# q and k loaded three tokens to a partition, and all loads in one order, in an attention and feed-forward kernel

## The chip, the cores and the metric

The kernel runs on one core of one Trainium2 chip. The time is that of the device, in microseconds (us), for one execution of the whole program: from inputs in HBM to the output in HBM. Besides plain timed runs there is one execution recorded by the hardware profiler, which gives the views quoted here. Engines are named as in the profile: PE does matmuls (and transposes), PEld is its loading of weights, DVE, ACT and POOL work on tensors, SP here only issues transfers (DMAs). ACT and POOL can issue DMAs too.

## The reference

Attention with a window of 128 tokens and four sink tokens, for 4 batches, 8 heads, 768 tokens and 64 dimensions a head, then a feed-forward layer over the 3,072 tokens. Cut to what matters:

```python
def _attn_ref(q, k, v, n_sink, window):      # n_sink 4, window 128
    scores = scale * np.matmul(q, k.transpose(0, 1, 3, 2))
    keep = is_sink | in_window               # rel >= 0 and rel < window
    scores = np.where(keep, scores, -1000000000.0)
    a = np.exp(scores - np.max(scores, axis=-1, keepdims=True))
    a = a / (np.sum(a, axis=-1, keepdims=True) + 1e-09)
    return np.matmul(a, v)

def _moe_ref(x, w_in, w_out, beta):          # x: 3072 x 512
    h = x @ w_in                             # 512 x 2048
    g = h * (1.0 / (1.0 + np.exp(-beta * h)))
    return g @ w_out                         # 2048 x 512
```

All inputs and the output are float32. The kernel works in bfloat16 between them.

## The kernel before

**Blocks and units.** The 3,072 tokens are cut into eight blocks of 384 (`HALF`; half a sequence). The attention of a block has four units, one for each pair of heads, so there are 32 units `u`; block `hb` is `u // 4`. The feed-forward layer works on whole blocks `T_`.

**Stages.** `load` brings q, k and v of a block into staging tiles (`stg`, two sets) in float32. `cast` makes bfloat16 of them: `x16` for q and k, `vaug` for v, which has a column of ones for the sum of the softmax. Stage T transposes q and k of a unit on PE (six 128 x 128 transposes, L417) and copies the result out of PSUM into `qkT` (L423, the copies appear at L306 for DVE and L308 for ACT); for the first block of a sequence it also copies the four sink columns of k into `kS` (L429). SC makes the scores of five or six 128 x 128 blocks (L468), ACT their exponentials (L478), POOL sets what lies outside the window to zero (L484), and DVE handles the sink blocks (L492). SS makes the scores against the sink tokens for the others (L502, L505). AV multiplies with `vaug` and `vS` (L530, L540) and divides (L544, L546). OT transposes back into `xT` (L558). H multiplies `xT` with `w_in` (L578), ACT takes the tanh (L582), DVE forms `g` (L584). O multiplies `g` with `w_out` over 16 steps (L596), the sum is copied to `osb` and stored by SP (L607).

**Who decides the order.** Each engine executes its instructions in the order in which the program adds them, and waits on semaphores. That order is worked out when the kernel is built: `Graph` keeps a modelled time for each engine and for the DMA engines (`free`, `dma_free`, `HOP` for a semaphore), each `add` has a modelled duration, and the loop at the end always adds the stage that can start earliest on PE, attention stages before feed-forward ones. `background` adds the next load when the modelled DMA backlog is under 3,000 ns, and the next cast when its data are due. `quickest` picks the engine for copies and for some casts, by the modelled times.

**Loads before.** In block 0, one DMA per head for q, k and v, q and v on SP and k on ACT, in the order q, k, v for each pair of heads. In the other blocks, one DMA of 256 KB for each 128 tokens of q, k or v, all heads, on SP. In both, token `c * 128 + p` lies in partition `p`, so each run in HBM is one token of one head, 64 float32 or 256 B. The weights come in eight chunks of 1 MB each (read as float32, written as bfloat16, 512 KB), issued by POOL: `w_in` after block 0, `w_out` after block 1. A DMA waits only until the tile that it writes is free.

**Names the prediction uses.** L352 issues loads of q, k and v, L361 those of the weights, L397 are the casts on POOL, L406 the copies of the sink rows of v.

Of the kernel before, what the change touches and what calls it, by code (L numbers as in the profile page):

```python
# [26 lines left out]
class Graph:  # L27
# [5 lines left out]
    HOP = 130  # L33

    def __init__(self):
        self.ops = []
        self.writers = {}
        self.readers = {}
        self.last_x = {}
        self.n_dma = 0  # L40
        self.n_eng = {e: 0 for e in self.ENGINES}
        self.free = {e: 0.0 for e in self.ENGINES}
        self.dma_free = 0.0

    def add(self, eng, fn, ns=0, r=(), w=(), x=(), dma=None):

        o = Op()
        o.eng, o.fn, o.dma = eng, fn, dma
        o.signal, o.count, o.waits, o.vc = False, 0, [], None
        o.seq = self.n_eng[eng]  # L50
        self.n_eng[eng] += 1
        deps = []
        for k in r:
            ws = self.writers.get(k)
            assert ws, k
            deps += [(p, True) for p in ws.values()]
        for k in w:
            deps += [(p, False) for p in self.readers.get(k, {}).values()]
            deps += [(p, False) for p in self.writers.get(k, {}).values()]
        for k in x:  # L60
            deps += [(p, False) for p in self.last_x.get(k, {}).values()]
        o.deps = deps
        who = ("dma", self.n_dma) if dma else eng
        if dma:
            self.n_dma += 1
        for k in r:
            self.readers.setdefault(k, {})[who] = o
        for k in w:
            self.writers[k] = {who: o}
            self.readers[k] = {}  # L70
        for k in x:
            self.last_x.setdefault(k, {})[eng] = o
        at = self.free[eng]
        for p, _ in deps:
            at = max(at, p.end + (0 if p.eng == eng and not p.dma else self.HOP))
        if dma:
            self.free[eng] = at + (1150 if eng == "gp" else 550)
            self.dma_free = max(self.dma_free, at + 900) + ns
            o.end = self.dma_free + 900
        else:  # L80
            o.end = self.free[eng] = at + ns
        self.ops.append(o)
        return o
# [144 lines left out]
def _program(nc, G, sb, ps, q, k, v, w_in, w_out, beta, out):  # L228
# [8 lines left out]
    hbeta = sb("hbeta", (128, NM), F32)  # L237
    xT = sb("xT", (128, 4, NTOK), BF16)
    w_in16 = sb("w_in16", (128, 4, DF), BF16)
    w_out16 = sb("w_out16", (128, NM, NOUT), BF16)  # L240
    stg = {n: sb(n + "_stage", (128, NK, H, D), F32, NSTG) for n in "qkv"}
# [14 lines left out]
    def add(eng, fn, ns, r=(), w=(), x=(), dma=None):  # L256
        return G.add(eng, fn, ns, r, w, x, dma)

# [71 lines left out]

    def beta_in():
        b_ = take(1)
        add("pe", lambda e: nc.tensor.transpose(P[:, b_[0], 0:NM], beta_st[:, :], ident32[:, :]), 30,
            r=["beta_st", "ident32"], x=[("B", b_[0])])
        add("dve", lambda e: e.tensor_scalar(hbeta[:, :], P[:, b_[0], 0:NM], 0.5, None, ALU.mult), 80,
            w=["hbeta"], x=[("B", b_[0])])
        give(b_)


    def load(hb, n, c, hp):  # L340

        b, t0, z = hb // 2, hb % 2 * HALF, hb % NSTG
        t = {"q": q, "k": k, "v": v}[n]
        if hp is None:
            src = t[b, :, t0 + c * 128:t0 + (c + 1) * 128, :].rearrange("h p d -> p h d")
            jobs = [(stg[n][z][:, c, :, :], src, [(n, z, c, i) for i in range(4)], f"d{n}{z}{c}", 262144)]
        else:
            jobs = [(stg[n][z][:, :, h, :], t[b, h, t0:t0 + HALF, :].rearrange("(c p) d -> p c d", p=128),
                     [(n, z, i, hp) for i in range(NK)] if h % 2 else [("first", n, hp)],
                     f"h{n}{h}", 98304) for h in (2 * hp, 2 * hp + 1)]  # L350
        for i, (dst, src, keys, sem, nbytes) in enumerate(jobs):
            add("act" if hp is not None and n == "k" else "sp", lambda e, dst=dst, src=src: e.dma_start(dst, src),  # L352
                nbytes / 265, w=[("stg",) + k_ for k_ in keys], dma=sem)

    def load_w(j):

        if j < 4:
            dst, src = w_in16[:, :, j * 512:(j + 1) * 512], w_in_src[:, :, j * 512:(j + 1) * 512]
        else:
            dst, src = w_out16[:, 4 * (j - 4):4 * (j - 3), :], w_out_src[:, 4 * (j - 4):4 * (j - 3), :]  # L360
        add("gp", lambda e: e.dma_start(dst, src), 1048576 / 380,  # L361
            w=[("w16", j)], dma=f"dw{j}")

    def cast(hb, n, c, hp):
        z = hb % NSTG
        cs = slice(0, NK) if c is None else slice(c, c + 1)
        hs = slice(0, H) if hp is None else slice(2 * hp, 2 * hp + 2)
        keys = [(i, j) for i in (range(NK) if c is None else [c]) for j in (range(4) if hp is None else [hp])]
        src = stg[n][z][:, cs, hs, :]
        r = [("stg", n, z) + k_ for k_ in keys]  # L370
        if hp is not None:
            r.append(("stg", "first", n, hp))
        if n == "v":
            dst = vaug[hb % NV][:, cs, hs, 0:D]
            w = [("v", hb % NV) + k_ for k_ in keys]
            r.append(("vones", hb % NV))
        else:
            dst = x16[n][hb % NX][:, cs, hs, :]
            w = [(n + "16", hb % NX) + k_ for k_ in keys]
        nc_, nh = (NK if c is None else 1), (H if hp is None else 2)  # L380
        opts = {}
        if n != "v" or nc_ == 1:
            opts["gp"] = pool_ns(nc_ * nh * D, nc_ * nh)
        if hb == 0:
            opts["dve"] = dve_ns(nc_ * nh * D)
            opts["act"] = act_ns(nc_ * nh * D) + 90
        eng = quickest(opts)
        if eng == "gp":
            if n == "v":
                dst, src = dst[:, 0, :, :], src[:, 0, :, :]  # L390
                patt = [[0, nh], [0, D]]
            else:
                dst, src = (a.rearrange("p c h d -> p c (h d)") for a in (dst, src))
                patt = [[0, nc_], [0, nh * D]]
                if nc_ == 1:
                    dst, src, patt = dst[:, 0, :], src[:, 0, :], patt[1:]
            fn = lambda e: e.affine_select(dst, src, patt, ALU.is_ge, 0.0, base=0, channel_multiplier=0)  # L397
# [3 lines left out]
        if n == "v" and hb % 2 == 0 and (hp == 3 or c == 0):  # L401
            z = hb // 2 % 2
            v0 = vaug[hb % NV][0:NSINK, 0, :, :].rearrange("p (a two) d -> p a two d", two=2)
            for hh in range(2):
                dst_ = vS[z][32 * hh:32 * hh + NSINK, :, :].rearrange("p (a two) d -> p a two d", two=2)[:, :, hh, :]
                add("dve", lambda e, dst_=dst_, hh=hh: e.tensor_copy(dst_, v0[:, :, hh, :]), 200,  # L406
                    r=[("vS", z)] + [("v", hb % NV, 0, j) for j in range(4)], w=[("vSd", z, hh)])


    def T(u):  # L410
# [4 lines left out]
        for i, n in enumerate("qk"):  # L415
            for c in range(NK):
# [3 lines left out]
                    mm_ns(128), r=[(n + "16", hb % NX, c, hp), "ident"], x=[("B", bs[0])])  # L420
        opts = {"dve": dve_ns(2 * HALF, 1.92), "act": act_ns(2 * HALF)}
        eng = quickest(opts)
        add(eng, copy_fn(eng, qkT[u % NT][:, :, :].rearrange("p a s -> p (a s)"), mp[:, 0:2 * HALF]), opts[eng],  # L423
            w=[("qkT", u % NT)], x=[("B", bs[0])])
        if hb % 2 == 0:
            ks = u % NKS
            for hh in range(2):
                rows = slice(64 * hh, 64 * hh + 64)
                add(eng, copy_fn(eng, kS[ks][rows, 32 * hh:32 * hh + NSINK], mp[rows, HALF:HALF + NSINK]), 70,  # L429
                    r=[("kS", ks)], w=[("kSd", ks, hh)], x=[("B", bs[0])])  # L430
# [85 lines left out]
    def av_keys(u):  # L516
        z = u % NE
        ks = {(p[0], z, p[1]) for ps in parts(where(u)[1]) for p in ps}
        return sorted(ks) + [("v", u // 4 % NV, c, u % 4) for c in range(NK)] + [("ES", z), ("vSd", u // 8 % 2, 1)]

    def AV(u):
# [4 lines left out]
        for m, ps in enumerate(parts(half)):  # L526
# [8 lines left out]
            for hh in range(2):  # L535
                c0 = (2 * m + hh) * (D + 1)
                for n, (kind, j, i, kb) in enumerate(ps):
# [4 lines left out]
                        r=[(kind, z, j), ("v", vz, kb % NK, hp)], x=[("B", bs[0])])  # L542
# [71 lines left out]
    def xl(hb):  # L614
        return [(hb, n, None, hp) for hp in range(4) for n in "qkv"] if hb == 0 else \
            [(hb, n, c, None) for c in range(NK) for n in "qkv"]

    LOADS = xl(0) + [0, 1, 2, 3] + xl(1) + [4, 5, 6, 7] + [x for hb in range(2, NSB) for x in xl(hb)]
    CASTS = [x for hb in range(NSB) for x in xl(hb)]
# [5 lines left out]
    def head(s):  # L625

        i = done[s]
        if s == "T":
            if i >= NU or i - NT + 4 >= min(done["SC"], done["SS"]):
                return None  # L630
            if n_cast[0] < (3 * i + 2 if i < 4 else 11 + 9 * (i // 4)):
                return None
            t = G.at([(n + "16", i // 4 % NX, c, i % 4) for n in "qk" for c in range(NK)])
# [7 lines left out]
        elif s == "AV":  # L641
            if i >= NU or i >= done["OT"] + NON or i >= min(done["SC"], done["SS"]) or n_cast[0] < (3 * i + 3 if i < 4 else 12 + 9 * (i // 4)):
# [33 lines left out]
    def background():  # L676
# [3 lines left out]
        while moved:  # L680
            moved = False
            i = done["load"]
            if i < len(LOADS) and G.dma_free <= now + BACKLOG:
# [6 lines left out]
                elif x[0] - NSTG < at_hb:  # L690
                    load(*x)
                    for c in range(NK) if x[2] is None else [x[2]]:
                        for hp in range(4) if x[3] is None else [x[3]]:
                            mark(("in",) + x, ("stg", x[1], x[0] % NSTG, c, hp))
# [3 lines left out]
            if i < len(CASTS):  # L698
                hb, n, c, hp = CASTS[i]
                t = G.at([("in",) + CASTS[i]])  # L700
                ok = done["T"] >= 4 * (hb - NX + 1) if n != "v" else done["AV"] >= 4 * (hb - NV + 2)
                if t is not None and ok and t <= now + AHEAD:
                    cast(hb, n, c, hp)
# [3 lines left out]
    add("sp", lambda e: e.dma_start(beta_st[:, :], beta.rearrange("(m p) -> m p", p=128)), 100, w=["beta_st"],  # L707
        dma="dbeta")
    consts()
    for x in xl(0):  # L710
        load(*x)
        for c in range(NK):
            mark(("in",) + x, ("stg", x[1], 0, c, x[3]))
    done["load"] = 12
# [66 lines left out]
```

## Time and profile before

| | us |
|---|---|
| median of 3 runs | 254.6 (253.06 to 254.76) |
| the profiled execution | 254.02 |
| its span, first to last instruction | 252.3 |
| PE busy in the span | 229.4 (91%) |
| ACT, DVE, POOL busy | 160.6, 121.8, 100.3 |
| DMA packets under 512 B, of all | 75,648 of 82,856 |
| bytes moved | 29.70 MB |

In the table by slices each digit is the busy share of one fortieth of the span, in tenths. PEclk is the clock that PE was granted, in tenths of full speed. A DMA share above 1 comes from packets that overlap on one DMA engine. In the chain of waits each line is a start, a length (both us) and what the end of the program was waiting for then. In the tables by group, a line names engine, operation, shapes and count, then busy time in us and mean ns of one, then the idle time of the engine ahead of it and what ended it.

### The profile page before, as it was taken

The numbers are of one execution on the slowest core, as the hardware profiler recorded it, in microseconds if no ns is written. First come the engines' busy times: TensorE is split into PE (matmuls) and PEld (weight loads), VectorE is DVE, ScalarE is ACT, GpSimd is POOL, SyncE is SP. The second block draws the span as 40 slices with busy tenths as digits, with TensorE's granted clock in tenths as the row PEclk, the third lists the DMA queues.
The fourth block names the chain that finished last, engine by engine and source line by source line (L and its number), as shares of the span: only waits on it lengthen the run. The fifth ranks groups of instructions, "written<-read, shape, count | busy, mean of one in ns | idle before, by whom it ended". The sixth has DMA issues, their size and how long they took to land.

```text
span 252.3 us, 5040 instructions
## 1 busy us (share of the span) xinstructions
PE 229.4 (91%) x1889; PEld 132.0 (52%) x1889; DVE 121.8 (48%) x274; ACT 160.6 (64%) x298; POOL 100.3 (40%) x204
## 2 busy tenths in 40 slices
PE   1588955899999999999999999999999999999994
PEld 0364632456565675656557565555555555555531
DVE  0484840244577567645657446533633533343320
ACT  1874873525998967899789776655644655554420
POOL 6582439464895989596298360000000000000000
PEclk9997997799999999999999999999999999999999
DMA  7999999969999899985011010111011011111112
GB/s 165 216 215 199 227 191 224 153 164 225 263 208 238 197 249 221 257 182 145 0 45 44 0 42 3 42 44 42 23 59 48 0 42 44 42 42 42 44 42 83
DMA packets 82856, 29.70 MB, mean 118 GB/s; under 512 B 75648, under 2 KB 79760, under 8 KB 82832
## 3 DMA queue, kind: packets, MB, share of 16 engines
q1 hardware_dynamic: 75408, 24.39, 39.5%
q0 software_dynamic: 4224, 4.19, 10.3%
q10 hardware_dynamic: 3200, 0.79, 1.4%
q8 instruction: 15, 0.25, 0.4%
q14 instruction: 9, 0.07, 0.1%
HBM read 27.27 MB, written 6.29 MB: 133 GB/s over the span
## 4 chain that ended last, share of the span: by engine, by line
PE 66%; SPq 11%; ACT 9%; DMA 7%; DVE 4%; issue 1%; POOL 1%; DVEq 0%
PE P L596 29%; PE P L578 26%; SPq L352 11%; ACT E L478 4%; DMA w_out<-in_moe_w_out_dram 4%; DMA v_stage<-in_v_dram 3%; PE P L540 2%; ACT t L582 2%; PE P L417 2%; PE P L558 2%; PE P L468 2%; DVE g L584 2%; DVE onorm L546 1%; ACT osb L308 1%; PE P L530 1%
## 5 line engine op out<-in xcount | busy, mean ns | idle before, releaser
L584 DVE SCALAR_TENSOR_TENSOR g<-t,P 128x384 bf16<-128x384 f32 x128 | 70.3, 554 | 81.9 <-ACT t L582 63.5
L582 ACT ACTIVATE t<-P,hbeta 128x384 f32<-128x384 f32 x128 | 74.2, 588 | 49.3 <-PE P L578 46.1
L596 PE MATMUL P<-w_out,g 128*128 128x512 bf16 x384 | 98.7, 383 | 6.5 <-DMA w_out<-in_moe_w_out_dram 5.6
L578 PE MATMUL P<-xT,w_in 128*128 128x384 bf16 x512 | 98.4, 330 | 0.4 <-ACT osb L308 0.4
L578 PEld LDWEIGHTS P<-xT,w_in 128*128 128x128 bf16 x512 | 49.2, 99 | 39.2 <-issue 1.5
L484 POOL TENSOR_SCALAR_AFFINE_SELECT E<-E 128x256 bf16<-128x256 bf16 (+1 forms) x112 | 52.0, 499 | 24.6 <-ACT E L478 24.4
L596 PEld LDWEIGHTS P<-w_out,g 128*128 128x128 bf16 x384 | 36.4, 98 | 42.5 <-ACT ES L505 3.6
L478 ACT ACTIVATE E<-P 128x768 bf16<-128x768 f32 x64 | 45.2, 765 | 9.9 <-PE P L468 9.4
L308 ACT ACTIVATE osb<-P 128x512 f32<-128x512 f32 x22 | 13.2, 602 | 14.6 <-PE P L596 14.6
L540 PE MATMUL P<-vaug,E 128*128 128x65 bf16 x352 | 19.8, 199 | 0.0
L397 POOL TENSOR_SCALAR_AFFINE_SELECT vaug<-v_stage 128x512 bf16<-128x512 f32 x21 | 14.0, 667 | 12.7 <-DMA v_stage<-in_v_dram 12.7
L540 PEld LDWEIGHTS P<-vaug,E 128*128 128x128 bf16 x352 | 17.7, 102 | 2.4 <-POOL E L484 0.3
L468 PE MATMUL P<-qkT 64*128 64x128 bf16 (+1 forms) x256 | 16.7, 254 | 2.4 <-ACT qkT L308 1.1
L546 DVE TENSOR_TENSOR onorm<-P,rden 128x384 bf16<-128x384 f32 x32 | 17.8, 558 | 1.1
L505 ACT ACTIVATE ES<-P 128x128 bf16<-128x128 f32 (+1 forms) x32 | 12.0, 400 | 3.9 <-PE P L502 3.6
L308 ACT ACTIVATE xT<-P 128x384 bf16<-128x384 bf16 x23 | 11.4, 500 | 4.5 <-PE P L558 4.4
L468 PEld LDWEIGHTS P<-qkT 64*128 64x128 bf16 x256 | 9.2, 99 | 9.6 <-issue 2.7
L558 PE MATMUL P<-ident,onorm 128*128 128x128 bf16 x96 | 10.9, 223 | 3.0 <-DVE onorm L546 2.3
L530 PE MATMUL P<-vS,ES 128*128 128x130 bf16 x64 | 13.3, 227 | 0.0
L544 DVE RECIPROCAL rden<-P 128x6 f32<-128x6 f32 x32 | 6.1, 191 | 14.0 <-PE P L540 13.7
L306 DVE COPY qkT<-P 128x768 bf16<-128x768 bf16 x20 | 10.8, 553 | 1.7 <-PE P L417 1.5
L558 PEld LDWEIGHTS P<-ident,onorm 128*128 128x128 bf16 x96 | 6.3, 98 | 9.8 <-DVE onorm L546 5.9
(46 smaller groups left out, 130.0 us busy)
## 6 DMA issues: line engine op xcount, KB each, us to landing
out_dram<-osb SPq DMA_DIRECT2D x24, 256.0 KB, 2.0
q_stage<-in_q_dram SPq DMA_DIRECT2D x21, 256.0 KB, 4.7
k_stage<-in_k_dram SPq DMA_DIRECT2D x21, 256.0 KB, 4.6
v_stage<-in_v_dram SPq DMA_DIRECT2D x21, 256.0 KB, 4.8
w_in<-in_moe_w_in_dram POOLq DMA_DIRECT2D x4, 512.0 KB, 8.5
w_out<-in_moe_w_out_dram POOLq DMA_DIRECT2D x4, 512.0 KB, 9.1
k_stage<-in_k_dram ACTq DMA_DIRECT2D x8, 96.0 KB, 4.0
q_stage<-in_q_dram SPq DMA_DIRECT2D x8, 96.0 KB, 3.4
```

The source lines that it names most:

```text
L308: return lambda e: e.activation(dst, src, AF.Copy, bias=0.0, scale=scale)
L352: add("act" if hp is not None and n == "k" else "sp", lambda e, dst=dst, src=src: e.dma_start(dst, src), nbytes / 265, w=[("stg",) + k_ fo ...
L468: add("pe", lambda e, dst=dst, kt=kt, kc=kc, rows=rows, q0=q0, nq=nq: e.matmul(dst, kt[rows, 1, kc:kc + 128], qkT[u % NT][rows, 0, q0:q0 + ...
L478: add("act", lambda e, src=src, dst_=dst_: e.activation(dst_, src, AF.Exp, bias=0.0, scale=SCALE), act_ns(256 * n), w=[(k_, z, j) for k_ i ...
L484: add("gp", lambda e, d=d, sg=sg, at_=at_: e.affine_select(d, d, [[0, 2 * len(at_)], [sg, 128]], ALU.is_ge, 0.0, base=min(sg, 0), channel_ ...
L540: e.matmul(A[:, c0:c0 + D + 1], E[z][:, i, hh, :], vaug[vz][:, kb % NK, 2 * hp + hh, :], start=a, stop=o, skip_group_check=True), 39,
L546: add("dve", lambda e: e.tensor_tensor(onorm[on][:, :, :, :].rearrange("p m h d -> p (m h) d"), av[:, :, 0:D], rden[on][:, :].unsqueeze(2) ...
L558: add("pe", lambda e, m=m: nc.tensor.transpose(mp[:, m * 128:(m + 1) * 128], onorm[on][:, m, :, :].rearrange("p h d -> p (h d)"), ident[:, ...
L578: add("pe", lambda e, c=c: e.matmul(hp, w_in16[:, c, m * 128:(m + 1) * 128], xT[:, c, t0:t0 + HALF], start=(c == 0), stop=(c == 3)), mm_ns ...
L582: add("act", lambda e: e.activation(tt[ti][:, :], hp, AF.Tanh, bias=0.0, scale=hbeta[:, m:m + 1]), act_ns(HALF) + 93, r=["hbeta"], w=[("t" ...
L584: add("dve", lambda e: e.scalar_tensor_tensor(gt[T_ % NG][:, m, :], tt[ti][:, :], 1.0, hp, ALU.add, ALU.mult), dve_ns(HALF), r=[("t", ti)] ...
L596: add("pe", lambda e, m=m: e.matmul(P[:, bk, :], gt[T_ % NG][:, m, t * 128:(t + 1) * 128], w_out16[:, m, :], start=(m == 0), stop=(m == NM ...
```

## The change

q and k are loaded with three neighbouring tokens to a partition: token `3 * p + j` lies in partition `p`, so a run in HBM is three tokens of one head, 768 B. Staging for q and k is laid out head by head (`H, NK, D`). The casts pick out the tokens of one `j`, so that each transpose gives every third token, and the copy out of PSUM writes them back in order, with a step of three elements. The sink copy for `kS` reads `qkT` instead of PSUM. v keeps its layout and its 256 B runs.

In block 0, q and k come in one DMA for each pair of heads (192 KB), then v in three DMAs of 256 KB; only the first k is on ACT, all else on SP. In the other blocks q is one DMA, k is one, v is three. AV of block 0 now waits for all eleven casts of the block. The load of beta moves from the first place on SP to behind six of these DMAs.

`ordered` gives all loads one order, weights too: each waits until the load that lies more than 1,600,000 bytes ahead of it has landed, whichever queue issues it. An early activation (`warm`) is added, and the constants of the model are changed. Keys of the planner follow the new layout.

```diff
-    HOP = 130
+    HOP = 180
...
-        self.free = {e: 0.0 for e in self.ENGINES}
+        self.free = {e: 800.0 for e in self.ENGINES}
...
-            self.dma_free = max(self.dma_free, at + 900) + ns
-            o.end = self.dma_free + 900
+            self.dma_free = max(self.dma_free, at + 1100) + ns
+            o.end = self.dma_free + 1000
...
-    stg = {n: sb(n + "_stage", (128, NK, H, D), F32, NSTG) for n in "qkv"}
+    stg = {n: sb(n + "_stage", (128, H, NK, D), F32, NSTG) for n in "qk"}
+    stg["v"] = sb("v_stage", (128, NK, H, D), F32, NSTG)
...
+    AHEAD_BYTES = 1600000
...
+        add("act", lambda e: e.activation(warm[:, :], ones[0:1, 0:1], AF.Exp, bias=0.0, scale=1.0), 1300,
+            r=["ones"], w=["warm"])
...
+    flight = []
+
+    def ordered(nbytes):
+
+        ahead, wait = 0, []
+        for key, b_ in reversed(flight):
+            ahead += b_
+            if ahead > AHEAD_BYTES:
+                wait = [key]
+                break
+        key = ("flight", len(flight))
+        flight.append((key, nbytes))
+        return wait, [key]
+
+    def load(hb, n, i):
 
         b, t0, z = hb // 2, hb % 2 * HALF, hb % NSTG
...
+        if n == "v":
+            src = v[b, :, t0 + i * 128:t0 + (i + 1) * 128, :].rearrange("h p d -> p h d")
+            dst, keys, ns = stg[n][z][:, i, :, :], [i], 262144 / 240
         else:
...
+            hs = slice(0, H) if i is None else slice(2 * i, 2 * i + 2)
+            src = {"q": q, "k": k}[n][b, hs, t0:t0 + HALF, :].rearrange("h (p j) d -> p h (j d)", j=NK)
+            dst = stg[n][z][:, hs, :, :].rearrange("p h j d -> p h (j d)")
+            keys, ns = ([i], 196608 / 350) if i is not None else (range(4), 786432 / 350)
+        wait, mine = ordered(dst.shape[0] * dst.shape[1] * dst.shape[2] * 4)
+        add("act" if hb == 0 and n == "k" and i == 0 else "sp", lambda e: e.dma_start(dst, src), ns, r=wait,
+            w=[("stg", n, z, j) for j in keys] + mine, dma=f"d{n}{z}{'' if i is None else i}")
...
-        add("gp", lambda e: e.dma_start(dst, src), 1048576 / 380,
-            w=[("w16", j)], dma=f"dw{j}")
...
+        wait, mine = ordered(1048576)
+        add("gp", lambda e: e.dma_start(dst, src), 1048576 / 380, r=wait, w=[("w16", j)] + mine, dma=f"dw{j}")
...
+        elif hb == 0:
+            hs = slice(2 * i, 2 * i + 2)
+            src = stg[n][z][:, hs, :, :].rearrange("p h j d -> p j h d")
+            dst = x16[n][hb % NX][:, :, hs, :]
...
+            src, dst = stg[n][z][:, :, i, :], x16[n][hb % NX][:, i, :, :]
...
-        opts = {"dve": dve_ns(2 * HALF, 1.92), "act": act_ns(2 * HALF)}
+        opts = {"dve": dve_ns(2 * HALF), "act": act_ns(2 * HALF)}
         eng = quickest(opts)
-        add(eng, copy_fn(eng, qkT[u % NT][:, :, :].rearrange("p a s -> p (a s)"), mp[:, 0:2 * HALF]), opts[eng],
+        add(eng, copy_fn(eng, qkT[u % NT][:, :, :].rearrange("p a (s j) -> p a j s", j=NK),
+                         mp[:, 0:2 * HALF].rearrange("p (a j s) -> p a j s", a=2, j=NK)), opts[eng],
             w=[("qkT", u % NT)], x=[("B", bs[0])])
...
-                add(eng, copy_fn(eng, kS[ks][rows, 32 * hh:32 * hh + NSINK], mp[rows, HALF:HALF + NSINK]), 70,
-                    r=[("kS", ks)], w=[("kSd", ks, hh)], x=[("B", bs[0])])
+                add(eng, copy_fn(eng, kS[ks][rows, 32 * hh:32 * hh + NSINK], qkT[u % NT][rows, 1, 0:NSINK]), 70,
+                    r=[("kS", ks), ("qkT", u % NT)], w=[("kSd", ks, hh)])
...
+        if hb:
+            return [(hb, "q", None), (hb, "k", None)] + [(hb, "v", c) for c in range(NK)]
+        return [(0, n, i) for i in range(4) for n in "qk"] + [(0, "v", c) for c in range(NK)]
...
-    CASTS = [x for hb in range(NSB) for x in xl(hb)]
+    CASTS = xl(0) + [(hb, n, i) for hb in range(1, NSB) for n in "qkv" for i in range(NK)]
...
-            if n_cast[0] < (3 * i + 2 if i < 4 else 11 + 9 * (i // 4)):
+            if n_cast[0] < (2 * i + 2 if i < 4 else 8 + 9 * (i // 4)):
...
-            if i >= NU or i >= done["OT"] + NON or i >= min(done["SC"], done["SS"]) or n_cast[0] < (3 * i + 3 if i < 4 else 12 + 9 * (i // 4)):
+            if i >= NU or i >= done["OT"] + NON or i >= min(done["SC"], done["SS"]) or n_cast[0] < 11 + 9 * (i // 4):
```

The list `LOADS` is as before: block 0, four chunks of `w_in`, block 1, four chunks of `w_out`, then the other blocks.

## The prediction

> **What bounds the kernel now.** I read the page's table by slices (6.3 us each) first, then the chain of waits, then busy times in stretches cut where the slices change.
>
> ```profile
> PE   1588955899999999999999999999999999999994
> ...
> PEclk9997997799999999999999999999999999999999
> DMA  7999999969999899985011010111011011111112
> ```
>
> PE is full from about slice 8 (50 us) to the end. Before that it has gaps and a lowered clock, and there the DMA engines are full. The stretches say it in us (PE, PEld, DVE, ACT, POOL busy, clock, DMA share, GB/s):
>
> ```profile
> 0.00:50.20 50.20, 33.36 (x286) 20.07 (x286) 21.51 (x52) 30.38 (x55) 27.91 (x64) 0.90 1.08 200
> 33.00:50.20 17.20, 10.68 (x100) 5.72 (x100) 3.73 (x9) 9.29 (x15) 9.26 (x19) 0.80 1.10 187
> 50.20:60.00 9.80, 9.77 (x78) 5.32 (x79) 3.51 (x10) 2.27 (x4) 5.83 (x11) 1.00 0.72 176
> 60.00:155.00 95.00, 92.68 (x1031) 58.18 (x1029) 58.16 (x145) 80.36 (x158) 66.57 (x131) 1.00 0.62 147
> ```
>
> Up to 50.2 us PE stands idle for 16.8 us, 6.5 of them between 33 and 50.2. From 50.2 to 155 us it is idle for 2.4. So what a load is worth is read from the first 50 us alone: later, other matmuls stand ready whenever a load is late. The chain names the loads:
>
> ```profile
> 16.95 5.81 SPq L352
> 22.80 4.35 SPq L352
> ...
> 29.72 7.90 DMA v_stage<-in_v_dram
> 37.68 0.67 POOL vaug L397
> ...
> 40.95 9.21 DMA w_out<-in_moe_w_out_dram
> 50.21 1.04 PE P L596 x4
> ```
>
> SP itself is held in issuing (5.8 and 4.4 us for one DMA), the last v chunk of block 1 lands at 37.6, and the last of w_out at 50.2, though only then the O stage of block 0 can finish. The queue of transfers, not an engine, ends this stage.
>
> **Loads: the runs.** Up to 50.2 us 10.02 MB were written: 4.19 of weights (eight chunks), 4.72 for blocks 0 and 1, and 1.05 for block 2 (four chunks that SP issued at 30.6, 31.7, 33.2 and 38.6, before or among the w_out chunks). Between 52.5 and 65 us, with no weights, q/k/v moved at 233 GB/s at a DMA share of 0.97. At that rate 5.77 MB take 24.8 us; with 2 us before the first bytes, the weights are left 50.2 - 2 - 24.8 = 23.4 us, 2.9 a chunk.
>
> ```profile
> q1 hardware_dynamic: 75408, 24.39, 39.5%
> 160.00:170.00 10.00, 10.00 (x55) 5.19 (x53) 3.92 (x8) 4.71 (x9) 0.00 (x0) 1.00 0.15 54
> ```
>
> A packet of that queue, nearly all 256 B, costs 0.395 x 252.3 x 16 / 75408 = 21.1 ns. No row has 768 B. Lower bound: as much as one of 256 B, 21.1, as it holds more bytes. Upper bound: as much as the three that it replaces, 63.3. The second row above has only output stores, 2 KB packets: 0.15 x 16 x 10 us / 264 packets = 91 ns. On the line between 256 B and 2 KB, 768 B lies at 41 ns, 0.65 of three; I take that, as it uses both neighbours. q and k of a block, 1.57 MB, then need 4.4 instead of 6.75 us; 2.25 and 6.75 are the ends. v keeps 3.4.
>
> **Loads: the order.** Each load now waits until what is more than 1.6 MB ahead has landed, so block 2 no longer mixes with w_out: 1.05 MB / 233 = 4.5 us. The last w_out chunk lands at 2 + 2 x (4.4 + 3.4) + 23.4 = 41 us instead of 50.2 (36.7 to 45.7 at the ends of the run price); w_in is in at 21.5, block 1 at 29.3 instead of 37.6.
>
> Moving seven of ACT's eight k DMAs to SP leaves one hardware queue. Two together moved 254 GB/s between 2 and 10 us, one 233 later: 0.6 us on 1.57 MB, or nothing. The Trainium skill, DMA: Bandwidth & Descriptors, section Rules for kernel authors, says that spreading DMAs over issuing engines adds no bandwidth, as all feed the same 16 engines; by the rule the price is zero, by the two stretches up to 0.6. I take zero here and keep 0.6. SP issues 11 DMAs for block 0 at about 0.53 us each instead of 17, so issuing ends near 6 us and doesn't limit. ACT loses 3.7 us of issuing, and its table load (1.28 us at 5.06) moves to about 1.4 by the new first activation.
>
> **PE in the first 50 us.** In the order in which the time falls:
> - FFN start. Its first matmul is at 20.3. Block 0's last v cast starts at 13.4 now; the loads would be in at about 9.8, and the first pair of q and k, one DMA each, issued at 0.8, about 1 us earlier. What remains is casts, copies and exps on ACT and DVE: eight casts at 0.53, four qkT copies at 0.8 to 0.95, four times 1.6 of exp, some 3 of masks and kS, 17 us on two engines. AV of the first pair now has to wait for all eleven loads, 9.8 us; it starts at 14.4 anyway. Of the 3.6 us by which loads are earlier I count 2.0 (between 0 and 3.6).
> - The gap. Of the 6.5 us idle between 33 and 50.2, what stays is where block 1 is paced by its four units on POOL (4 masks a unit, 1.94 us, 7.8 in all) and ACT (1.5 + 0.43 a unit). Transposes near 29 and w_out chunks at 32, 35, 38 and 41 give PE 7 us of attention and about 3 to 5 of L596 in the 11 us until then. I count 4.5 saved, 2 left (0 to 6.5).
> - The clock, in stretches of 2.5 us:
>
> ```profile
> 37.50:40.00 2.50, 0.59 (x3) 0.32 (x4) 0.00 (x0) 1.08 (x3) 2.31 (x4) 1.00 1.22 201
> 40.00:42.50 2.50, 1.18 (x11) 0.40 (x10) 0.00 (x0) 1.51 (x2) 2.49 (x6) 0.69 1.25 248
> 42.50:45.00 2.50, 2.50 (x20) 1.52 (x18) 0.00 (x0) 0.00 (x0) 1.16 (x3) 0.50 1.24 211
> 45.00:47.50 2.50, 2.22 (x16) 0.92 (x14) 1.11 (x3) 1.95 (x3) 0.77 (x2) 0.50 1.22 198
> ```
>
> Behind a stretch with 0.59 us of work PE runs at 0.69 and 0.50: 1.18 x 0.31 + (2.50 + 2.22) x 0.5 = 2.7 us lost. Half is saved, 1.4.
>
> **What is added on engines.** The qkT copy writes every third element:
>
> ```profile
> L306 DVE COPY qkT<-P 128x768 bf16<-128x768 bf16 x20 | 10.8, 553 | 1.7 <-PE P L417 1.5
> L308 ACT ACTIVATE qkT<-P 128x768 bf16<-128x768 bf16 x12 | 10.0, 829 | 1.5 <-PE P L417 1.5
> L584 DVE SCALAR_TENSOR_TENSOR g<-t,P 128x384 bf16<-128x384 f32 x128 | 70.3, 554 | 81.9 <-ACT t L582 63.5
> ```
>
> DVE packed: 768 elements 553 ns, 384 (the xT copy) 358, so 0.51 ns an element and 162 fixed. At L584's rate, (554 - 162) / 384 = 1.02, it is 945. Bounds 553 and 945; I take 945. The Trainium skill, VectorE: DVE Perf Modes, section What auto-detection actually checks, speaks against the change: two 16-bit results a cycle need step 1. Its table of cycles makes an estimate of 925 ns, and no row here has the strided copy; the sum by it is the same to 0.4 us. On DVE 20 x 0.39 = 7.8 us more, of which 6 fall into 60 to 155, where DVE has 37 idle: hidden. If DVE were full it would cost the 6. ACT keeps 829 or less, as its row shows no faster packed form. POOL's casts of q/k go from 615 to v's 667, 42 x 0.05 = 2.2 us, in 28 us of idle. The kS copies now read qkT and wait for their own engine's copy, 153 ns each; SS and the exps queue behind: at most 32 x 0.1. I take +0.5 for all these.
>
> SP's new waits stand ahead of loads and, after 50 us, of output stores; four osb buffers cover some us. POOL's stand ahead of casts and masks: see the second rival. Planner constants reorder everything else; no row prices that, and I put it in the range as 1 us either way.
>
> **Sum.** -2.0 - 4.5 - 1.4 + 0.5 = -7.4. The profiled execution took 254.0 (span 252.3 and 1.7 around it): 246.6. It lies 0.6 below the median of 254.6: about **247.0** in the median. Changes under 1% (252.1 to 257.1) are what a measurement can't tell from none.
>
> **Rivals.**
> - *Only the order helps.* 768 B cost 63 ns, or the runs are cut into 256 B packets after all: w_out at 45.7, half of the first three terms, 254.6 - 3.9 + 0.5 = 251.2. For it: no row shows such a packet. Against: 2 KB costs 91, not eight times 21.1.
> - *POOL's queue paces the loads: slower.* A weight chunk takes 8.5 to 9.1 us from issue to landing now, and the new wait lets two be in flight. At 8.8, eight chunks need 4 x 8.8 = 35 us instead of 23.4, w_out ends at 52.7, its last issue is at 43.9 instead of 41.0, and the masks of block 1 are behind it on POOL. The 16.9 us from that issue to the first L578 of block 1 (57.8) then end 3 us later: 254.6 + 3 + 0.5 = 258. It decides from about 8 us a chunk. Against: 8.8 includes q/k/v sharing the engines; two chunks alone are 5.9.
> - *ACT takes the copies.* If all go to ACT, 15 x 0.81 = 12 us join its 80.4 of 95: 97%, and masks and tanh wait. With 6 us lost the gain is nearly gone: 253.2. Against: DVE has room.
>
> **How the numbers follow.** Forecast 0.60 (243 to 249.5), order only 0.15, ACT 0.11, POOL 0.14. Faster by over 1%: 0.60 + 0.15 = 0.75 and a little of ACT, 0.76; within: 0.11; slower: 0.13. The range goes from 241.5 (all of 3.6, 6.5 and 2.7) to 254, which leaves out POOL and the ends of the others.
>
> **What would show it.** Packets on q1 near 45,500 instead of 75,408 (24,576 of q and 21,504 of k go, a third of 48,384 comes); last w_out landing at 41; first L578 near 18; idle PE from 33 to 50 us under 3; DVE's qkT copy near 945 ns. I'm wrong if w_out chunks still take over 8 us from issue, or POOL's masks wait behind them, or PE gets new idle after 60 us with ACT ahead of it.

## The result, and the profile after

The changed kernel takes 264.3 us (261.97 to 265.0), the kernel before 253.83 in the same session: a ratio of 1.0395, with an interval of 1.0315 to 1.0475. It is slower by 4%, where 247.0 was forecast. Here and below a time is the median of all executions, while a ratio compares means and leaves out executions more than 1.5% above the fastest of their kernel. The profiled execution has a span of 263.2 us, 10.9 more than before.

The first view is the page's table by slices of the changed kernel (6.6 us each here).

```profile
PE   1688977597899699988999999999999999999995
...
DMA  6799995999999990970010101011111111111112
```

Counted from slice 0, PE has gaps up to slice 18 now (125 us); before, it was full from slice 8 (50 us). The DMA engines have a gap in slice 6 (39 to 46 us), while the weights are still on their way. The stretches say where the time is (columns as before: length, PE, PEld, DVE, ACT, POOL, clock, DMA share, GB/s):

```profile
10.00:15.00 5.00, 3.85 (x32) 1.68 (x31) 4.20 (x8) 4.97 (x12) 3.46 (x8) 1.00 0.45 75
33.00:50.20 17.20, 11.94 (x136) 6.84 (x134) 6.79 (x14) 13.66 (x20) 12.80 (x24) 1.00 0.93 161
60.00:155.00 95.00, 85.47 (x892) 51.16 (x890) 62.14 (x130) 82.53 (x143) 62.25 (x119) 0.98 0.57 144
```

From 60 to 155 us PE is idle for 9.5 us, against 2.3 before. This is the stretch in which the prediction let other matmuls stand ready. Between 33 and 50.2 it is idle for 5.3 instead of 6.5. The idle time after 60 us is not the whole loss: over the whole span PE's idle time rose from 22.9 to 28.4 us, and its busy time from 229.4 to 234.8 for the same 1,889 matmuls; why these got longer isn't shown. The row from 10 to 15 us shows the DMA engines at 0.45 (0.94 before): they run dry in the stage that they were to end. Two groups of the page (engine, operation, shapes, count, then busy us and mean ns) name the engines' new work:

```profile
L313 ACT ACTIVATE qkT<-P 128x768 bf16<-128x768 bf16 x20 | 28.8, 1486 | 1.1 <-PE P L427 1.1
...
L311 DVE COPY qkT<-P 128x768 bf16<-128x768 bf16 x12 | 17.4, 1448 | 0.4 <-PE P L427 0.4
```

The copy that puts q and k back in order takes 1,486 ns on ACT, which had 829, and 1,448 on DVE, which had 553. In all, 46.2 us of copies where there were 20.8. In the page's shares of the chain that ended last, by engine and by line, they are the largest item behind the two feed-forward matmuls, 9% and 2% of the span; before, no such copy was among the fifteen largest, and ACT had 9% in all.

```profile
PE 64%; ACT 21%; DVE 6%; DMA 4%; issue 1%; POOL 1%; SPq 0%; DVEq 0%; ACTq 0%
PE P L589 28%; PE P L607 26%; ACT qkT L313 9%; ACT E L489 6%; PE P L551 3%; DMA w_out<-in_moe_w_out_dram 3%; PE P L569 2%; ACT t L593 2%; PE P L479 2%; DVE g L595 2%; DMA k_stage<-in_k_dram 2%; DVE qkT L311 2%; DVE onorm L557 2%; ACT ES L516 1%; PE P L427 1%
```

The chain of waits of the changed kernel, cut to the stage that the prediction was about (start, length, what the end waited for):

```profile
35.18 3.90 ACT qkT L313 x3
...
42.33 1.89 POOL E L495 x4
44.21 6.62 DMA w_out<-in_moe_w_out_dram
50.89 1.46 PE P L607 x3
```

Three copies in a row lead it, then exps and the masks of a unit, then the last chunk of w_out, which POOL issues only behind these masks. It lands at 50.8 us; before, 50.2. So two things went wrong, and the experiments have to say how far they belong together: the copies became slower than was priced, and the faster loads didn't bring the weights in any earlier.

### The profile page after: what moved, and what is told of

Same layout as the page of the kernel before. It is cut to its first block, busy times and chain, and to the rows that moved or that the text cites. A ratio compares the mean times of both kernels' runs of the same rounds, so it can differ in the third digit from the quotient of the medians.

```text
span 263.2 us, 4995 instructions
## 1 busy us (share of the span) xinstructions
PE 234.8 (89%) x1889; PEld 132.6 (50%) x1889; DVE 132.6 (50%) x267; ACT 179.1 (68%) x307; POOL 100.5 (38%) x202
## 3 DMA queue, kind: packets, MB, share of 16 engines
q1 hardware_dynamic: 44912, 24.98, 35.6%
## 4 chain that ended last, share of the span: by engine, by line
PE 64%; ACT 21%; DVE 6%; DMA 4%; issue 1%; POOL 1%; SPq 0%; DVEq 0%; ACTq 0%
PE P L589 28%; PE P L607 26%; ACT qkT L313 9%; ACT E L489 6%; PE P L551 3%; DMA w_out<-in_moe_w_out_dram 3%; PE P L569 2%; ACT t L593 2%; PE P L479 2%; DVE g L595 2%; DMA k_stage<-in_k_dram 2%; DVE qkT L311 2%; DVE onorm L557 2%; ACT ES L516 1%; PE P L427 1%
## 5 line engine op out<-in xcount | busy, mean ns | idle before, releaser
L589 PE MATMUL P<-xT,w_in 128*128 128x384 bf16 x512 | 100.0, 333 | 0.4 <-DVE rden L555 0.4
L589 PEld LDWEIGHTS P<-xT,w_in 128*128 128x128 bf16 x512 | 50.0, 100 | 39.2 <-issue 3.3
L313 ACT ACTIVATE qkT<-P 128x768 bf16<-128x768 bf16 x20 | 28.8, 1486 | 1.1 <-PE P L427 1.1
L551 PE MATMUL P<-vaug,E 128*128 128x65 bf16 x352 | 20.9, 203 | 0.2 <-ACT vaug L313 0.2
L313 ACT ACTIVATE osb<-P 128x512 f32<-128x512 f32 x20 | 12.1, 604 | 12.3 <-PE P L607 12.3
L479 PE MATMUL P<-qkT 64*128 64x128 bf16 (+1 forms) x256 | 17.8, 251 | 2.2 <-ACT E L489 0.9
L551 PEld LDWEIGHTS P<-vaug,E 128*128 128x128 bf16 x352 | 18.5, 104 | 2.3 <-issue 0.6
L557 DVE TENSOR_TENSOR onorm<-P,rden 128x384 bf16<-128x384 f32 x32 | 17.8, 558 | 1.1
L311 DVE COPY qkT<-P 128x768 bf16<-128x768 bf16 x12 | 17.4, 1448 | 0.4 <-PE P L427 0.4
L516 ACT ACTIVATE ES<-P 128x128 bf16<-128x128 f32 (+1 forms) x32 | 12.9, 409 | 1.0 <-PE P L513 0.8
```

The source lines that it names most:

```text
L311: return lambda e: e.tensor_copy(dst, src)
L313: return lambda e: e.activation(dst, src, AF.Copy, bias=0.0, scale=scale)
L479: add("pe", lambda e, dst=dst, kt=kt, kc=kc, rows=rows, q0=q0, nq=nq: e.matmul(dst, kt[rows, 1, kc:kc + 128], qkT[u % NT][rows, 0, q0:q0 + ...
L551: e.matmul(A[:, c0:c0 + D + 1], E[z][:, i, hh, :], vaug[vz][:, kb % NK, 2 * hp + hh, :], start=a, stop=o, skip_group_check=True), 39,
L557: add("dve", lambda e: e.tensor_tensor(onorm[on][:, :, :, :].rearrange("p m h d -> p (m h) d"), av[:, :, 0:D], rden[on][:, :].unsqueeze(2) ...
L589: add("pe", lambda e, c=c: e.matmul(hp, w_in16[:, c, m * 128:(m + 1) * 128], xT[:, c, t0:t0 + HALF], start=(c == 0), stop=(c == 3)), mm_ns ...
```

## The experiments

The theories: COPY (the step on the writing side makes the copies slow, and that makes the kernel slow), ORDER (the loads' new waits do), PLAN (an order that the planner made with wrong durations does), and, for the missing gain of the loads, POOL, MIX and CHANCE. Each ratio is to the kernel before, run beside it.

**1. The same copy, walked in the other order.**

```diff
-        add(eng, copy_fn(eng, qkT[u % NT][:, :, :].rearrange("p a (s j) -> p a j s", j=NK),
-                         mp[:, 0:2 * HALF].rearrange("p (a j s) -> p a j s", a=2, j=NK)), opts[eng],
+        add(eng, copy_fn(eng, qkT[u % NT][:, :, :].rearrange("p a (s j) -> p a s j", j=NK),
+                         mp[:, 0:2 * HALF].rearrange("p (a j s) -> p a s j", a=2, j=NK)), opts[eng],
```

> The changed kernel with one edit: the copy out of PSUM walks the same elements in the other order, so that it reads with a step of 128 elements from PSUM and writes qkT packed (six bytes at a time without gaps). Result the same, order of all instructions the same. Theory COPY (the step of three on the writing side is what makes the copy 1448 ns on DVE and 1486 on ACT): the copy falls to 800 to 950 ns on both, and the time to 254 to 257. Theory ORDER (the waits of the loads make the kernel slow, the copy matters little): 262 to 265 whatever the copy takes. If the copy stays near 1450 ns, the step is costly on either side.

252.51 us, ratio 0.9943 (0.9919 to 0.9967). The groups of this kernel:

```profile
L313 ACT ACTIVATE qkT<-P 128x768 bf16<-128x768 bf16 x20 | 15.9, 822 | 2.7 <-PE P L427 2.6
...
L311 DVE COPY qkT<-P 128x768 bf16<-128x768 bf16 x12 | 11.4, 953 | 0.4 <-PE P L427 0.4
```

and its stretch, to be read against the last row of the same view above:

```profile
60.00:155.00 95.00, 91.56 (x997) 56.67 (x1009) 64.90 (x139) 82.38 (x153) 66.79 (x129) 1.00 0.56 140
```

The same elements are moved with the same order of instructions. With the step on the reading side ACT takes 822 ns and DVE 953, PE's idle time from 60 to 155 us falls from 9.5 to 3.4, and 11.8 us are gone. (The row has 997 matmuls for 1,009 weight loads: some matmul records are missing, so the idle time is at most 3.4.) ORDER falls as the cause of the loss.

**2. No reordering at all.**

```diff
+        add(eng, copy_fn(eng, qkT[u % NT][:, :, :].rearrange("p a s -> p (a s)"), mp[:, 0:2 * HALF]), opts[eng],
```

> The changed kernel with the reordering left out: the copy out of PSUM reads and writes packed, so q and k stand in qkT in the order of the transposes (j, then p) and the scores are those of other tokens; all sizes and the order of all instructions are the same. Theory COPY: DVE 554 ns and ACT 829 ns as before, 250 to 254, since everything else of the change then stands against before alone. Theory ORDER: 261 to 265.

251.61, ratio 0.991 (0.9883 to 0.9938), DVE 553 ns and ACT 822. Against the first experiment, DVE's 0.4 us for each of its twelve copies is worth 0.9 us at most. So the reordering, rightly written, is nearly free, and all else of the change stands within 2 to 3 us of the kernel before.

**3. The change without the loads' waits.**

```diff
-        return wait, [key]
+        return [], [key]
```

> The changed kernel with the waits of the loads left out (a load waits only until its tile is free, as before); the copies keep their step of three. Theory COPY: 261 to 266, the copy stays at 1450 ns. Theory ORDER: 251 to 256, with the weight chunks issued by POOL earlier than 11.9, 14.9, 17.6, 20.6 and w_out landing near 43 instead of 50.8.

262.0, ratio 1.0315 (1.029 to 1.0339): as COPY said. Without the waits the kernel is 2.3 us faster, of the 10.5; the planner's order changes with them, so the waits themselves may be worth less.

**4. The kernel before with the change's copy alone.** The edit is the copy of the diff, in the kernel before.

> The kernel of before with only the copy of the change: the copy out of PSUM writes with a step of three, so q and k stand in qkT in another token order and the scores are those of other tokens; sizes and the order of all instructions are those of before. Theory COPY: DVE and ACT near 1450 ns, 261 to 268. Theory ORDER: 254 to 256, what 32 longer copies cost where they are hidden.

263.12, ratio 1.0348 (1.0304 to 1.0392). The group and the stretch:

```profile
L306 DVE COPY qkT<-P 128x768 bf16<-128x768 bf16 x20 | 28.3, 1443 | 0.5 <-PE P L417 0.4
```

```profile
60.00:155.00 95.00, 85.01 (x925) 52.86 (x936) 65.19 (x133) 79.43 (x146) 63.21 (x124) 1.00 0.61 143
```

The old loads, the old order, no waits: the copy alone brings the 1,443 ns, most of the idle time of PE (10 us in this row, of which some 3 may be its eleven missing matmul records), and 9.4 of the 10.5 us. Undone in one kernel and done alone in the other, it accounts for the loss both times. COPY is shown.

**5. Work or order?** The planner had 865 ns for DVE and 700 for ACT. In this run it is told what the copies take.

```diff
-        opts = {"dve": dve_ns(2 * HALF), "act": act_ns(2 * HALF)}
+        opts = {"dve": 1450, "act": 1470}
```

> The changed kernel with its copy that writes with a step, and the planner told what it takes: 1450 ns on DVE and 1470 on ACT instead of 865 and 700. Only the order of the instructions and the choice of the engine change. Theory PLAN (the copies are slow, but what costs 10 us is that PE's fixed order puts matmuls behind them too soon): 254 to 258, with idle PE from 60 to 155 us at 3 to 5 instead of 9.5. Theory WORK (the added 20 to 27 us on ACT and DVE can't be hidden in any order): 260 to 265.

258.49, ratio 1.0185 (1.0143 to 1.0227), PE idle from 60 to 155 us for at most 7.2 us. Between both theories: of the 10.5 us of loss 4.4 stay (258.49 against 254.06 beside it), and some 6 come back with another order and another split of the copies (16 on each engine instead of 20 on ACT). This is one order, and experiments 12 to 17 show that orders alone lie up to 5 us apart, so the 6 us are no price of the plan. The engines never were full (ACT 82.5 of 95). That a longer copy is a late operand, and that PE's fixed order decides how many matmuls wait behind it, fits this; it is a reading, not shown by itself.

**6. Where is the gain of the loads?** Experiment 1 without the waits (the edit of experiment 3).

> The kernel of the first experiment (copy reads with a step, writes packed; 252.5) without the waits of the loads. What is open is why the loads, whose packets cost what was predicted, gained 1 to 2 us instead of 8. Theory POOL (the weight chunks are issued by POOL, which stands at waits, masks and casts, so the DMA engines run dry near 11, 38 and 43 us and w_out lands at 47.4 instead of 41): without the waits the chunks are issued earlier, w_out lands at 44 or before, and the time falls to 248 to 251. Theory MIX (the order is worth what was predicted, 4.5 us of transfers of block 2 kept behind w_out): without it block 2 mixes in again and the time rises to 254 to 256. Both small: 251.5 to 253.5.

253.5, ratio 0.9958 (0.9925 to 0.9991): "both small". MIX doesn't show. POOL wasn't put to the test: the condition was not met, as POOL issued the last chunk at 42.8 us here and at 41.6 in experiment 1. With or without the waits the kernel is about 1 us faster than before.

**7. The constants alone,** in the kernel before.

```diff
-    HOP = 130
+    HOP = 180
...
-        self.free = {e: 0.0 for e in self.ENGINES}
+        self.free = {e: 800.0 for e in self.ENGINES}
...
-            self.dma_free = max(self.dma_free, at + 900) + ns
-            o.end = self.dma_free + 900
+            self.dma_free = max(self.dma_free, at + 1100) + ns
+            o.end = self.dma_free + 1000
...
-                nbytes / 265, w=[("stg",) + k_ for k_ in keys], dma=sem)
+                nbytes / 240, w=[("stg",) + k_ for k_ in keys], dma=sem)
```

> The kernel of before with only the planner's constants of the change (HOP 180, engines free at 800 ns, the DMA latencies, loads at 240 GB/s instead of 265); no load, copy or wait is changed, only the order of the instructions. If the constants are neutral, as the prediction assumed to 1 us either way: 253 to 255. If they are what pays in the first experiment: 250 to 252.5, and the loads paid nothing. If they cost: over 255, and the loads paid more than 1.5 us.

252.97, ratio 0.995 (0.993 to 0.9969). The planner's constants alone, with the old loads, give as much as the first experiment; the gain there need not be one of the loads.

**8. True durations with the packed write:** experiment 1, and the planner is told its copy's times.

```diff
-        opts = {"dve": dve_ns(2 * HALF), "act": act_ns(2 * HALF)}
+        opts = {"dve": 950, "act": 820}
```

> The kernel of the first experiment (252.5) with the planner told 950 ns on DVE and 820 on ACT, as measured there, instead of 865 and 700. Theory PLAN: 250 to 252, some tenths to 2 us less. Theory WORK: 252 to 253.

252.79, ratio 0.9947 (0.9926 to 0.9967): as experiment 1.

**9 to 11. More ahead, more in flight, a truer plan.** All three start from 8.

```diff
-    AHEAD_BYTES = 1600000
+    AHEAD_BYTES = 2700000
...
-    BACKLOG, AHEAD = 3000, 300
+    BACKLOG, AHEAD = 5500, 300
```

That is the second of them. The first leaves the waits out (the edit of experiment 3) and has a backlog of 8,000. The third keeps waits and backlog and sets more durations:

```diff
-        add("gp", lambda e: e.dma_start(dst, src), 1048576 / 380, r=wait, w=[("w16", j)] + mine, dma=f"dw{j}")
+        add("gp", lambda e: e.dma_start(dst, src), 1048576 / 350, r=wait, w=[("w16", j)] + mine, dma=f"dw{j}")
...
-        opts = {} if hb == 0 and n != "v" else {"gp": pool_ns(size)}
+        opts = {} if hb == 0 and n != "v" else {"gp": 660}
...
-                opts = {"gp": 1150, "dve": dve_ns(512)}
+                opts = {"gp": 1150, "dve": 470}
```

and in the same way 210 instead of 70 for the kS copies.

> The copy that reads with a step, true durations in the plan (252.8 with the waits), no waits of the loads, and the planner may issue loads 8,000 ns ahead of the modelled DMA engines instead of 3,000, so that POOL meets the weight chunks before casts and masks that wait. Theory POOL (late issue by POOL is what eats the gain of the loads): the last w_out chunk is issued before 38 and lands before 45, 248 to 251. Theory FULL (PE has other work by then; when w_out lands between 45 and 50 makes no difference): 251.5 to 254 although w_out lands earlier. Mixed traffic that delays block 1 instead would give over 254.

253.31, ratio 0.9978 (0.9945 to 1.0011). The last chunk of w_out was issued at 32.5 us, and no chunk took over 11.0, so all were in by 43.5, some 7 us before the kernel before had it, and the time didn't move. The stretches show two effects that cancel:

```profile
0.00:20.00 20.00, 7.35 (x55) 3.76 (x55) 7.15 (x16) 9.09 (x19) 9.27 (x29) 1.00 1.02 216
20.00:33.00 13.00, 10.31 (x85) 6.77 (x86) 5.41 (x14) 8.26 (x17) 10.31 (x18) 1.00 1.21 247
33.00:50.20 17.20, 16.00 (x152) 9.43 (x151) 9.83 (x19) 15.62 (x27) 6.75 (x15) 1.00 1.12 238
```

The gap of PE from 33 to 50.2 us is 1.2 us, against 6.5 before and 4.6 in experiment 1, as POOL has it. But PE had only 7.35 us of work in the first 20 (9.98 before, 11.95 in 8), and the feed-forward part began at 27.9 instead of 20.3; the first two chunks were issued at 4.5 us, among the loads of block 0, which may be why. So the time alone doesn't decide between POOL and FULL, and FULL's reason, that PE has other work by then, doesn't fit the gap that closed.

> The same kernel with the waits kept, but with 2.7 MB in flight instead of 1.6 and loads issued up to 5,500 ns ahead: POOL waits less at its weight chunks. Theory POOL: no dips of the DMA engines at 11, 38 and 43 us, w_out in by 44, 248 to 251. Theory FULL: 251.5 to 253.5.

248.74, ratio 0.9783 (0.9741 to 0.9825): faster by 2.2%, with w_out in at 45.7. This is the gap, and the stage from 50 us on, in this kernel, and then the latter in experiment 1:

```profile
33.00:50.20 17.20, 15.39 (x157) 8.85 (x155) 7.39 (x16) 13.26 (x22) 12.69 (x25) 1.00 1.20 241
50.00:62.00 12.00, 11.84 (x106) 7.10 (x105) 7.61 (x15) 8.50 (x20) 9.66 (x17) 1.00 1.07 271
```

```profile
50.00:62.00 12.00, 9.81 (x69) 5.35 (x68) 3.79 (x8) 7.60 (x18) 6.47 (x11) 1.00 0.93 260
```

From 50 to 62 us PE (first column after the length) is busy for 11.84 us here and for 9.81 there, with DVE and POOL busier too. But experiment 9 has 11.82 there and gains nothing in the end, and the kernel before has 11.77, so this hole doesn't explain 248.7. In this trace the gap accounts for it: PE is idle for 1.8 us from 33 to 50.2, where it was for 6.5 before, and these 4.7 us are what the span became shorter by (252.3 to 247.6). The first 33 us and the rest together are as before.

> The same kernel with the waits as in the change, and more of the plan's durations set to what the traces show: kS copies 210 instead of 70, POOL's casts 660 instead of 617, DVE's sink masks 470 instead of 598, weight chunks at 350 GB/s instead of 380. Theory PLAN (waits of PE come from an order made with wrong durations): 250 to 252. If these small ones don't matter: 252 to 253.5.

258.96, ratio 1.0185 (1.0139 to 1.0232), against 252 to 253.5 expected at worst. The truer durations gave an order that is 6 us slower. It put a cast of v on POOL ahead of the weights,

```profile
10.19 0.90 POOL L384 DMA_DIRECT2D w_in<-in_moe_w_in_dram  x1
...
12.61 0.66 POOL L407 TENSOR_SCALAR_AFFINE_SELECT vaug<-v_stage 128x512 bf16<-128x512 f32 x1
...
15.78 0.76 POOL L384 DMA_DIRECT2D w_in<-in_moe_w_in_dram  x1
19.93 0.76 POOL L384 DMA_DIRECT2D w_in<-in_moe_w_in_dram  x1
...
46.96 0.76 POOL L384 DMA_DIRECT2D w_out<-in_moe_w_out_dram  x1
```

and the last chunk went out at 47 and landed near 53 (out at 40.1 in experiment 8). That POOL's queue can pace the loads is seen here, in another kernel than the change. How much of the 6 us it is stays open: PE's idle time from 60 to 155 us rose too, from 3.7 in experiment 8 to 6.3. PLAN in its simple form (truer is faster) falls.

**12 and 13. What an order is worth.** Experiment 1 with `HOP` at 170 and at 190; nothing is built differently but the order.

```diff
-    HOP = 180
+    HOP = 170
```

> The kernel of the first experiment (copy reads with a step; 252.5) with the modelled semaphore delay at 170 ns instead of 180: nothing is different but the order that the planner works out. Theory CHANCE (orders that differ by nothing that matters lie several us apart, so 1 to 4 us between two packed kernels say nothing about loads): this run and the next lie 2 us or more apart or away from 252.5. If orders are steady: both 252 to 253.5, and differences of 2 us between other experiments mean something.

254.39, ratio 1.0016 (0.9987 to 1.0046).

> The same with 190 ns. CHANCE: 2 us or more from 252.5 or from the run with 170. Steady: 252 to 253.5.

255.3, ratio 1.0042 (1.0018 to 1.0065). Kernels that differ by nothing but the order lie 252.5, 254.4 and 255.3. CHANCE holds, by 2.8 us in 13 and just short of its 2 us in 12: the mean is 254.1, the time before, and the 1.3 us of experiment 1 can't be put down to the loads.

**14 and 15. The halves of the edit that gave 248.7:** 14 has only `AHEAD_BYTES` at 2,700,000, 15 only the backlog of 5,500, both on top of experiment 8.

> The kernel that read with a step and knew the copies' durations (252.8), with 2.7 MB in flight instead of 1.6 and the modelled backlog as in the change, 3,000 ns: one half of the edit that gave 248.7. Theory POOL (POOL and SP waiting on loads in flight is what ate the gain): 248 to 250.5. If the modelled backlog did it: 252 to 253.5.

252.12, ratio 0.9914 (0.9885 to 0.9944).

> The other half: 1.6 MB in flight as in the change, loads issued up to 5,500 ns ahead of the modelled DMA engines. If the backlog did it: 248 to 250.5. Theory POOL: 252 to 255, as POOL then meets its weight chunks earlier and stands at their waits longer, ahead of masks and casts.

255.21, ratio 1.0026 (0.9996 to 1.0056). Neither half does it alone; the room in flight by itself does no more than experiment 8's 252.8 within the intervals.

**16 to 18. The best version and the change in other orders.** 16 and 17 are experiment 10 with `HOP` at 170 and 190, 18 is the change itself with `HOP` at 170.

> The kernel that gave 248.7 (packed write, true durations, 2.7 MB in flight, backlog 5,500 ns) with the modelled semaphore delay at 170 instead of 180. If its lead is one of a lucky order: 251 to 256, as the two such runs before lay 2 to 3 us off. If room in flight is what pays: 247 to 250.5.

250.3, ratio 0.9844 (0.98 to 0.9889).

> The same with 190. Lucky order: 251 to 256. Room in flight: 247 to 250.5.

253.61, ratio 0.9949 (0.991 to 0.9988). With room in flight the three orders give 248.7, 250.3 and 253.6, mean 250.9; without it, in the plan of experiment 1, 254.1. By the ratios that is 0.986 against 1.000. The sets overlap (0.9949 here, 0.9943 there), so part of 248.7 is a fortunate order, and what the room is worth by itself stays open. The gap of PE from 33 to 50.2 us doesn't overlap: it is 1.8, 0.8 and 1.6 us with room, and 4.6, 4.3 and 3.9 in experiments 1, 12 and 13.

> The change as it is, with 170 instead of 180. If what it loses were a bad order: 253 to 260. If the copy's 1450 ns is the cause, as the packed copies and the strided copy alone say: 261 to 267.

265.23, ratio 1.0444 (1.0378 to 1.051). The change's loss stands in another order.

## Why the prediction was wrong, point by point

**The failed step is the price of the qkT copy.** "Bounds 553 and 945; I take 945" for DVE, and "ACT keeps 829 or less, as its row shows no faster packed form". Measured: 1,448 and 1,486. In the sum the copy was part of "+0.5 for all these"; alone in the kernel before it costs 9.4 us (experiment 4). The upper bound came from L584's rate, 1.02 ns an element, as if that were the slowest that the engine goes. For ACT the row of the packed copy was taken for the stepped one too. What costs is the writing: with the reordering on the reading side both engines take what the prediction had, 953 and 822 (experiment 1). The rule that it drew on (the Trainium skill, VectorE: DVE Perf Modes, section What auto-detection actually checks), two 16-bit results a cycle only for step 1, fits 953 (925 by the estimate from the page's table), not 1,448. No row of the trace before had such a write; the upper bound needed a reason and had none.

**"Hidden" was the second error.** The cover named was 37 us of idle DVE between 60 and 155 us. Busy sums don't tell whether a late operand holds PE: DVE and ACT stayed at 62 and 83 of 95, and PE still lost 7 us there. That its instructions are in one fixed order is the likely reason; the trace puts PE's waits in that stretch down to DVE for 4.7 us (3.7 of it the division `onorm`, L557) and to ACT for 4.4 (2.3 of it the copies into qkT and kS), so by the profile the delay reaches PE mostly through what follows the copies. The third rival came nearest (copies on ACT make PE wait), but its price, 6 us off a gain of 7.4, was too small and it counted on a full ACT.

**The gain of the loads, 7.9 us in three terms, was not there.** The packet count came as predicted (44,912 on q1, 45,456 by the count), and so did the price of a 768 B packet: taking what v and the stores cost out of q1's 35.6% leaves, as an estimate, 42 to 47 ns, 41 predicted. The rate: from 2.5 to 7.5 us, with almost nothing but q and k in the changed kernel, 304 GB/s against 253 before on two queues; a gain, though less than 357, the rate behind 4.4 us a block. The landing failed: w_out at 50.8 instead of 41. The slow copies are a part of that, as masks wait for them and weights for masks: with the packed write it is 47.4 (experiment 1). The term that was missing is the issue. POOL sends the weights between its masks and casts, at 11.9, 14.9, 17.6, 20.6, and then 30.9 to 44.2; the DMA engines fell to 0.45 meanwhile. That was weighed as a rival, with too narrow a mechanism (8.8 us from issue to landing, measured 5.5 to 6.7) and a price of 3 us.

The three terms one by one. *The gap* (4.5 saved, 2 left): from 33 to 50.2 us PE is idle for 5.3 us in the change and 4.6 in experiment 1, so 1 to 2 were saved. Where the weights do come earlier the term is there, 4.7 saved and 1.8 left in experiment 10; it failed by the late issue, not by its size. *The start* (2.0): the first matmul of the feed-forward part is at 21.6 instead of 18, and at 20.1 with the packed copy (20.3 before), so the term was zero. ACT is busy for 14.1 of the first 20 us in experiment 1; that casts, copies and exps pace block 0, and not loads, fits this but wasn't tried. *The clock* (1.4): it was 1.00 from 33 to 50.2 us, but 0.66 from 50 to 55 and 0.91 from 80 to 100 instead. With the packed write, in experiments 1 and 10, it is 1.00 throughout, but so it is in experiment 4 with the old loads and the slow copy; that the loads bring it isn't shown, and experiment 1 gains no more than 1.3 us in all. The prediction read the lowered clock as following a stretch of little work; in experiment 10 PE does nothing from 12.5 to 15 us and has 1.00 behind it, so that alone isn't enough.

The sum had a slip of its own, without weight: 254.6 less 7.4 is 247.2, not 247.0.

**What was right:** POOL's casts of q and k (654 to 675 ns, 667 predicted), the table load at 1.3 us, the first transpose about 1 us earlier (4.4 instead of 5.3), and the sentence on what would prove it wrong: new idle of PE after 60 us. "I put it in the range as 1 us either way" for the planner's constants was too narrow: orders alone differ by 3 to 5 us (experiments 12, 13, 16 and 17), and one order was 6 us slower (experiment 11).

## What to carry to other kernels

When a layout is undone in a copy, put the step on the side that reads, and measure the copy alone before pricing it; the rate of another instruction's row is no upper bound for an access that no row has. In a kernel whose order is fixed at build, don't price a longer operation by the idle time of its engine; ask which matmul stands behind it. Before a gain of 1% from such a planner is put down to a mechanism, the same kernel should be run in two or three orders that differ in nothing else.

## What the runs showed of the hardware

A write of two-byte elements to SBUF with a step of three cost about the same on both engines, 1,448 ns on DVE and 1,486 on ACT for 768 elements, 1.8 times ACT's packed time (829). Reading the same elements from PSUM with a step of 128 cost ACT nothing (822 against 829) and DVE 400 ns (953 against 553). The Trainium skill, SBUF — State Buffer, section Door 1: The DMA port swizzle, says in a note on lines of 16 bytes that a step of up to eight bf16 elements is free; the writes here, six bytes apart, were not, and the measurement decides. Why the writes are slow was not tried further.
